# The second layer of two blocks merged into the column transform's block products

## The chip, the cores and the metric

The kernel runs on one core of one Trainium2 chip. Times are device microseconds of that core. The program of before was run twice: 861.01 and 860.78 us, median 860.89 us. Engines are named as in the profile: PE (matrix products) and PEld (its weight loads), DVE (vector), ACT (scalar), POOL (GpSimd), SP (here only an issuer of DMAs).

## The reference, cut to what matters

For 2,048 rows x of 640 columns, xn = layernorm(x), and the result is a sum of three terms:

```
a = xn @ Wd_re.T ;  b = xn @ Wd_im.T           # transform along the 640 columns
A = Ws_re @ a - Ws_im @ b                      # transform along the 2,048 rows, real part
h = gelu(xn @ w1 + b1)                         # 640 -> 1,536, tanh form of gelu
B = h @ w2 + b2                                # 1,536 -> 640
out = x + A + B
```

All inputs are float32. The kernel computes the transforms with the matrices that it is given; it does the row transform first, P = Ws_re @ xn and Q = Ws_im @ xn, and then the column transform, A = P @ Wd_re.T - Q @ Wd_im.T.

## The kernel before

**Products.** Each float32 operand is split into a high part of type fp32r and the rest. `product` (L272 to L274) issues three matmuls: high x high, high x low, low x high. A split is one ACT copy (high, L160) and one DVE subtraction (low, L161). Every matmul has a stationary 128x128 piece and 512 moving columns. Work goes by four blocks t = 0 to 3 of 512 rows.

**First part, the two-layer term (MLP).** For each block there are 12 units i of 128 hidden features. `hidden` (L292) does 15 matmuls into bank g mod 3, `gelu` (L305 to L311) activates on ACT and splits the result, and `output` does 5 x 3 matmuls with the split W2 of that unit into five banks, which add up over the 12 units. PE's order is hidden(g+2), output(g). In block 0 each unit also brings in and splits its piece of W1 and W2 (`load_w1`, four DMAs on SP, `load_w2`, one DMA; `prep_w1`, `prep_w2`), three buffers deep. `background` lays the layernorm of the next block between the units: rows of x are loaded, normalised by DVE, stored to the DRAM tensor xs (16 DMAs a block), read back turned (`load_z`, four DMAs, after all stores), transposed by DVE and split (`prep_xt`). `prep_w` makes the forms of the column transform's matrices on ACT and DVE, stores them from ACT's own DMA queue to DRAM (`wits`), three steps for each of five 128-column groups. At the end of a block b2 is added on ACT, DVE turns the result, and GpSimd adds it to x (L337); the sum waits in DRAM (`ys`).

**Second part, the row transform.** It uses seven block products in place of eight, in sequence stages of 14 entries (7 products w, 2 entries each). For each entry, `form` splits the moving operand three entries ahead into one of three places of the tile `as`, so ACT first waits until PE has done the entry that used the place.

**Third part, the column transform.** For two blocks at a time, a stage of 21 entries (7 products, 3 entries each: two pairs of 128-row chunks and one single). Its operands are the sums u and v (the two transforms of the block's rows), in seven combinations, against the forms of the Fourier matrices from `wits`, which `load_g` brings in ahead, in the last stage up to 19 forms deep. The order of the stages is: row transform of all blocks (first half), of (1,3) and (1,0), column transform of 3 and 0, row transform of (1,1) and (1,2), column transform of 1 and 2. What stands beside each entry on DVE, ACT and SP is written out by entry number in `beside` and `hidden_beside`: sums between operands, turned outputs, loads.

The order on each engine is that in which the program is written. A DMA carries one of eight semaphores, given in turn to the DMAs of SP and ACT, and is not issued until the earlier DMA with that semaphore has landed.

Of the kernel before, what the change touches and what calls it, by code (L numbers as in the profile page):

```python
# [15 lines left out]
P = 128  # L16
# [10 lines left out]
def kernel(  # L27
# [13 lines left out]

# [38 lines left out]
    NC = TB // P  # L80

# [16 lines left out]
    forms_c = dram.tile([NK, P, 2, 7 * P], F32, name="forms_c")  # L98
    parts2 = dram.tile([NT, 4, P, 2, TB], F32, name="parts2")
# [74 lines left out]
    xt = {}  # L174

    def load_x(c, eng=nc.sync):
        xt[c] = row_tile(f"x{c}")
        eng.dma_start(xt[c], x[c * P : (c + 1) * P])  # L178
# [42 lines left out]
    def new_xt(t, j):  # L221
        XT[j] = mr.tile([P, 2, TB], F32R, tag="xt", bufs=ND, name=f"xt{t}_{j}")
# [14 lines left out]
    def prep_xt(t, j):  # L237
        new_xt(t, j)
        split(XT[j][:, 0], XT[j][:, 1], zt.pop(j))
# [3 lines left out]
    def load_w1(i, eng=nc.sync):  # L243
        if i >= NF:
            return
        t = early.tile([P, ND, P], F32, tag="w1r", bufs=3, name=f"w1r{i}")
# [5 lines left out]
    def load_w2(i, eng=nc.sync):  # L252
        if i >= NF:
            return
        t = early.tile([P, D], F32, tag="w2r", bufs=3, name=f"w2r{i}")
# [24 lines left out]
    def hidden(g):  # L280
        i = g % NF
# [8 lines left out]
        for n, (j, k) in enumerate(steps):  # L290
            a, b = kinds[k]
            nc.tensor.matmul(  # L292
                acc, W1[i][:, a, j * P : (j + 1) * P], XT[j][:, b], start=n == 0, stop=n == len(steps) - 1
# [5 lines left out]
    FIRST += [(1, 1), (4, 0), (4, 2), (2, 1), (3, 1), (4, 1)]  # L299

# [116 lines left out]
    blocks = [(0, t) for t in range(NT)] + [(1, t) for t in (NT - 1, *range(NT - 1))]  # L417
# [74 lines left out]
    entries = [(*st, w, u) for st in stages for w in range(NW) for u in range(2 if st[0] == "s" else 3)]  # L492
# [4 lines left out]
    def form(n):  # L497
# [7 lines left out]
        else:  # L505
            names, which = MOV[w]
            src = sums[what[which], names[u]]
            if u < 2:
# [90 lines left out]
    warms = [early.tile([P, TB], F32R, tag="w1r", bufs=3, name=f"warm{k}") for k in range(3)]  # L599
# [18 lines left out]
    load_w2(0)  # L618
    nc.sync.dma_start(b1c, b1.rearrange("(i p) -> p i", p=P))
    load_w2(1)  # L620
    load_w2(2)

    for tag, size, keys in PLACES:
        t = place(tag, (P, size // 4))
# [42 lines left out]
    for j in range(ND):  # L667
        split(XT[j][:, 0], XT[j][:, 1], tacc[j])
    load_w1(3)
    load_w1(4)  # L670
# [5 lines left out]
    prep_w2(0)  # L676
    prep_w1(2)
    load_w2(3)
    load_w1(5)


    def background(t, i):

        if t == 1 and i == 0:
# [5 lines left out]
        if t + 1 < NT:  # L690
            c0 = (t + 1) * NC

            s = 2 if t == 0 else 0
            if t == 0 and i < 2:
                ln_apply(2 * i)
                ln_apply(2 * i + 1)
# [616 lines left out]
```

## Time and profile before

| | |
|---|---|
| median of two runs | 860.89 us |
| span of the profiled execution | 858.6 us |
| difference, outside first and last instruction | 2.3 us |
| PE busy | 850.2 us, 3,747 matmuls |
| DVE, ACT, POOL busy | 624.1, 335.7, 21.0 us |
| DMA | 152.34 MB, mean 177 GB/s |

The profiled execution is a further one, which has a span and no time of its own; the median stands 2.3 us above that span. A row of a group gives engine and line, operation, out<-in, shapes and count, then busy time and mean ns of one, then idle time ahead and what ended it. A row in order of time gives start, duration, engine, line, operation and count of merged neighbours. SPq is SP's DMA queue: the time is that of issuing, not of the transfer. A row of a stretch (A:B) gives its length, then busy time of PE, PEld, DVE, ACT and POOL with counts, the granted clock, the DMA engines' share and GB/s.

### The profile page before, as it was taken

What the parts mean: (1) busy time and instruction counts of PE and PEld (TensorE: products, weight loads), DVE (VectorE), ACT (ScalarE), POOL (GpSimd) and SP (SyncE); (2) the same over time, 40 slices, a digit from 0 to 9 for tenths busy, and PEclk for the clock granted to TensorE, in tenths of its full rate; (3) what the DMA queues carried; (4) which work ended last, traced back from release to release, by engine and by line L of the source; (5) the groups of instructions that cost most, each with busy time, mean ns of one, the idle gap of its engine ahead of it and who ended that gap; (6) DMA issues with size and microseconds to landing.
All of it is one profiled execution on the core that took longest, in us unless ns stands there. A gap on an engine that the chain in (4) does not pass through costs nothing.

```text
span 858.6 us, 10232 instructions
## 1 busy us (share of the span) xinstructions
PE 850.2 (99%) x3747; PEld 703.1 (82%) x3747; DVE 624.1 (73%) x792; ACT 335.7 (39%) x468; POOL 21.0 (2%) x22
## 2 busy tenths in 40 slices
PE   8999999999999999999999999999999999999997
PEld 6888888888888888888888888888888888888885
DVE  7554555366443678989989787998977998885687
ACT  7354434255333555443434344232322423223241
POOL 0000300030003000000000000000000000000000
PEclk9999999999999999999999999999999999999999
DMA  6656476875457984949753659954765879804364
GB/s 184 198 164 175 97 176 189 215 153 174 141 165 169 319 358 86 218 105 216 167 151 86 184 159 266 237 127 107 176 186 172 260 177 230 313 19 177 123 170 105
DMA packets 208625, 152.34 MB, mean 177 GB/s; under 512 B 82368, under 2 KB 182976, under 8 KB 208064
## 3 DMA queue, kind: packets, MB, share of 16 engines
q1 hardware_dynamic: 196336, 138.98, 62.4%
q10 hardware_dynamic: 12240, 12.72, 4.2%
q8 instruction: 29, 0.48, 0.2%
q14 instruction: 20, 0.16, 0.1%
HBM read 108.67 MB, written 42.99 MB: 177 GB/s over the span
## 4 chain that ended last, share of the span: by engine, by line
PE 98%; DMA 0%; DVE 0%; SPq 0%; issue 0%; ACT 0%; DVEq 0%; ACTq 0%
PE banks L273 26%; PE banks L272 26%; PE banks L274 26%; PE banks L292 19%; DMA x<-in_A_x_dram 0%; PE banks L635 0%; DVE st L185 0%; SPq L178 0%; DVE yo L1278 0%; DVE mv L186 0%; DVE xp L208 0%; ACT mv L192 0%; DVE mv L194 0%; DVE mv L195 0%; DVE mv L197 0%
## 5 line engine op out<-in xcount | busy, mean ns | idle before, releaser
L274 PE MATMUL banks<-as,xab 128*128 128x512 f32 x407 | 158.4, 389 | 0.0
L272 PE MATMUL banks<-as,xab 128*128 128x512 f32 x407 | 158.3, 389 | 0.0
L273 PE MATMUL banks<-as,xab 128*128 128x512 f32 x407 | 158.3, 389 | 0.0
L160 ACT ACTIVATE as<-r 128x1024 fp32r<-128x1024 f32 x80 | 85.0, 1062 | 173.1 <-PE banks L274 148.6
L161 DVE TENSOR_TENSOR as<-r,as 128x1024 fp32r<-128x1024 f32 x80 | 97.2, 1216 | 38.9 <-ACT as L160 38.9
L292 PE MATMUL banks<-xt,xab 128*128 128x512 f32 x420 | 99.1, 389 | 0.0
L311 DVE TENSOR_TENSOR hs<-ab,hs 128x512 fp32r<-128x512 f32 x48 | 36.5, 760 | 78.5 <-ACT hs L309 78.5
L292 PEld LDWEIGHTS banks<-xt,xab 128*128 128x128 f32 x420 | 78.7, 188 | 16.5 <-DVE xt L161 0.2
L272 PEld LDWEIGHTS banks<-as,xab 128*128 128x128 f32 x407 | 76.4, 188 | 16.0
L273 PEld LDWEIGHTS banks<-as,xab 128*128 128x128 f32 x407 | 76.4, 188 | 15.9
L274 PEld LDWEIGHTS banks<-as,xab 128*128 128x128 f32 x407 | 76.4, 188 | 15.8
L272 PE MATMUL banks<-as,xc 128*128 128x512 f32 x224 | 87.1, 389 | 0.0
L273 PE MATMUL banks<-as,xc 128*128 128x512 f32 x224 | 87.1, 389 | 0.0
L274 PE MATMUL banks<-as,xc 128*128 128x512 f32 x224 | 87.1, 389 | 0.0
L305 ACT ACTIVATE ab<-banks,b1c 128x512 f32<-128x512 f32 x48 | 33.0, 689 | 96.3 <-PE banks L292 91.8
L160 ACT ACTIVATE as<-rt 128x1024 fp32r<-128x1024 f32 x32 | 34.0, 1063 | 70.6 <-PE banks L274 57.9
L292 PE MATMUL banks<-xt,as 128*128 128x512 f32 x240 | 57.0, 389 | 0.0
L292 PEld LDWEIGHTS banks<-xt,as 128*128 128x128 f32 x240 | 45.0, 188 | 9.4
L272 PEld LDWEIGHTS banks<-as,xc 128*128 128x128 f32 x224 | 42.0, 188 | 8.8
L273 PEld LDWEIGHTS banks<-as,xc 128*128 128x128 f32 x224 | 42.0, 188 | 8.7
L274 PEld LDWEIGHTS banks<-as,xc 128*128 128x128 f32 x224 | 42.0, 188 | 8.7
L272 PE MATMUL banks<-hs,xc 128*128 128x512 f32 x120 | 46.7, 389 | 0.0
(170 smaller groups left out, 1365.5 us busy)
## 6 DMA issues: line engine op xcount, KB each, us to landing
raw<-in_A_dft_seq_re_dram SPq DMA_DIRECT2D x64, 256.0 KB, 5.9
raw<-in_A_dft_seq_im_dram SPq DMA_DIRECT2D x64, 256.0 KB, 5.4
wit<-wst ACTq DMA_DIRECT2D x20, 384.0 KB, 3.5
ws<-wit SPq DMA_DIRECT2D x15, 384.0 KB, 4.4
x<-in_A_x_dram SPq DMA_DIRECT2D x16, 320.0 KB, 4.3
xs<-x SPq DMA_DIRECT2D x64, 80.0 KB, 1.8
xo<-in_A_x_dram SPq DMA_DIRECT2D x16, 320.0 KB, 6.1
forms_ab<-xab SPq DMA_DIRECT2D x4, 1280.0 KB, 5.9
```

The source lines that it names most:

```text
L160: nc.scalar.activation(h, s, AF.Copy)
L161: nc.vector.tensor_tensor(l, s, h.bitcast(F32), op=ALU.subtract)
L272: nc.tensor.matmul(acc, wh, mh, start=first, stop=False, skip_group_check=goes_on)
L273: nc.tensor.matmul(acc, wh, ml, start=False, stop=False, skip_group_check=goes_on)
L274: nc.tensor.matmul(acc, wl, mh, start=False, stop=last, skip_group_check=goes_on)
L292: nc.tensor.matmul(acc, W1[i][:, a, j * P : (j + 1) * P], XT[j][:, b], start=n == 0, stop=n == len(steps) - 1)
L305: nc.scalar.activation(a, acc, AF.Gelu_apprx_tanh, bias=b1c[:, i : i + 1])
L311: nc.vector.tensor_tensor(hs[:, 1], a, hs[:, 0].bitcast(F32), op=ALU.subtract)
```

## The change

Blocks 0 and 1 no longer have an `output` in the first part. Their gelu results stay float32 and go to a new DRAM tensor hd, two units together (512 KB), from ACT's queue (`keep`). In the last column-transform stage, which now belongs to blocks 0 and 1 (the order of the last row blocks is turned about), the 12 units take part as six more 128-row chunks of contraction in each of the seven products: the first six units stand beside u, the other six beside v, and the pieces of w2 beside the real and the imaginary matrix. The stage has 42 entries, six for each product: three as before, and three with two chunks of units each (`merged_entry`).

The raw w2 is loaded during the last row-transform stage (`load_raw_w2`); the forms of w2 that the seven products need are made in the stage itself, high parts by ACT, low parts and the sums between by GpSimd (`w2_form`, `w2_sums`), in eight places (`wt`). x is added to the two blocks by loading it as the start of the output tile, b2 by GpSimd (`bias_rows`). The forms of the Fourier matrices there have 6 places in place of 19.

In the first part, blocks 0 and 1 have 15 matmuls for a unit. W1 has six raw buffers; W2's pieces are loaded and split from the end of block 1 on, one for each unit of block 2. `background` is a table by block and unit.

```
+    def keep(g, acc):
+        t, i = divmod(g, NF)
+        if i % 2 == 0:
+            HT["kept"] = mr.tile([P, 2, TB], F32, tag="hs", bufs=3, name=f"hu{g}")
+        h = HT["kept"]
+        nc.scalar.activation(h[:, i % 2], acc, AF.Gelu_apprx_tanh, bias=b1c[:, i : i + 1])
+        if i % 2:
+            nc.scalar.dma_start(hd[t, i // 2], h)
...
+            (0, 0): [lambda: apply(0, 1), lambda: stats(4)],
+            (0, 1): [lambda: apply(2, 3), lambda: stats(5), lambda: rows_in(8, 9, 10, 11)],
+            (0, 2): [lambda: stats(6, 7)],
+            (0, 3): [lambda: ln_scale(4, 4), lambda: apply(4, 5, 6, 7), lambda: load_z(1)],
...
+            (0, 10): [lambda: prep_x(1, 3, 4), lambda: rows_in(12, 13, 14, 15)],
...
+    w_steps = [(1, i) for i in (1, 2, 3, 10, 11)] + [(2, i) for i in (0, 1, 2, 3, 4, 5, 5, 6, 7, 7)]
...
+    for g in range(NM * NF):
+        t, i = divmod(g, NF)
+        acc = (acc0, acc1)[g] if g < 2 else hidden(g)
+        if t == 0:
+            prep_w1(i + 3)
+            load_w1(i + 6)
+        keep(g, acc)
+        beside_mlp(t, i)
...
+    def bias_rows(dst, c0, c1):
+        nc.gpsimd.tensor_tensor(dst, dst, A["b2"][:, c0:c1].unsqueeze(1).to_broadcast([P, NB, c1 - c0]), op=ALU.add)
...
+        for tag, n in (("xc01", 5), ("xab3", 3)):
+            r = place(tag, (P, n, 2, 3 * P))
+            A["wt"] += [r[:, k] for k in range(n)]
...
+    def w2_form(k):
+        if k >= NW * NH:
+            return
+        w, f = divmod(k, NH)
+        t = A["wt"][k % len(A["wt"])]
+        WT[w, f] = t
+        at = 0
+        for half, c0, n in W2_PARTS[w]:
+            src = w2_cols(f, half, c0, n)
+            hi, lo = (t[:, a, at * P : (at + n) * P].rearrange("p (c q i) -> p c q i", q=Q, i=B) for a in range(2))
+            nc.scalar.activation(hi, src, AF.Copy)
+            pool_add(lo, src, hi.bitcast(F32), ALU.subtract)
+            at += n
+        w2_sums(k + 4)
...
+            post = [lambda k=k: w2_form(k) for k in w2_steps(n)]
+            post += {
...
+                1: [lambda: bias_rows(ya, 0, DQ)],
+                4: [lambda: bias_rows(yo[tb, 4], 4 * B, DQ)],
...
+    def w2_steps(n):
+        if n < 4:
+            return (2 * n, 2 * n + 1)
+        w, u = divmod(n - 1, HU + NH // 2)
+        return [8 + NH * w + 2 * (u - HU) + k for k in range(2)] if u >= HU else []
```

More of the change, by code (lines that the diff above doesn't have):

```diff
@@ L254, in load_w2 @@
             return
[L255 removed]
+        t = row_tile(f"w2r{i}")
         w2r[i] = t
@@ L491, with parts_of @@
             stages.append(("y", (blocks[k - 1][1], blk[1])))
-    entries = [(*st, w, u) for st in stages for w in range(NW) for u in range(2 if st[0] == "s" else 3)]
+    HU = ND // 2 + 1
+    def parts_of(kind, what):
+        return 2 if kind == "s" else HU + NH // 2 if what == stages[-1][1] else HU
+    entries = [(*st, w, u) for st in stages for w in range(NW) for u in range(parts_of(*st))]
+    units = {}
     SRC = ("cr1", "cr2", "ci1", "cr1", "cr2", "cr1", "ci2")
@@ L1249 @@
         b = blocks.index(what) if kind == "s" else b
-        count = NW * (2 if kind == "s" else 3)
+        count = NW * parts_of(kind, what)
         for n in range(first, first + count):
```

379 lines of the change are left out of this document (278 added, 101 removed).

## The prediction

> **What bounds the kernel now.** I read the page first, then PE in order of time, the chain of waits, the DMA issue queue, and last the groups and stretches that give prices. Page, PE's first hidden units, chain:
>
> ```profile
> span 858.6 us, 10232 instructions
> PE 850.2 (99%) x3747; PEld 703.1 (82%) x3747; DVE 624.1 (73%) x792; ACT 335.7 (39%) x468; POOL 21.0 (2%) x22
> ```
> ```profile
> 12.13 10.56 PE L292 MATMUL banks<-xt,xab 128*128 128x512 f32 x45
> ```
> ```profile
> 66.89 3.40 PE banks L292 x15
> ...
> 852.85 0.24 PE banks L274
> ```
>
> PE is busy for 850.2 of 858.6 us. Hidden units start at 12.13, the last matmul stands at 852.85, and between them the chain stays on PE: 15 matmuls of one hidden unit take 3.40 us, 0.227 us each. No wait inside can be removed. Only fewer matmuls make this kernel shorter, and every new wait of PE adds its full length. The runs' median is 860.89, 2.3 us above this execution's span; I add these 2.3 at the end. Two per cent (17.2 us, about what a measurement here tells from no change) means 843.7 and 878.1.
>
> **What is removed.** The second layer of blocks 0 and 1 costs 2 x 12 chunks x 5 column blocks x 3 = 360 matmuls. In its place each of the seven products gets six more chunks of contraction: 18 block columns x 6 x 3 = 324. So 36 go, 36 x 0.227 = **-8.2 us**. Removing all else that PE lacks to 100% would bring 8.4 more, 16.6 together: faster by over 2% is out of reach.
>
> **The first block.** Before, 30 matmuls stood between two hidden units (6.8 us); now 15, in blocks 0 and 1. Unit 10 of block 0 is wanted at 12.13 + 10.56 (three units) + 7 x 3.40 = 46.5 us. Its W1 column must have come by then. It comes through SP's queue (issue start, time, count; then microseconds to landing, SP's waits, the two halves of the split, and the stretch):
>
> ```profile
> 0.74 1.83 SPq L178 DMA_DIRECT2D x<-in_A_x_dram  x4
> 5.30 5.61 SPq L250 DMA_DIRECT2D w1r<-in_B_w_dram  x12
> ...
> 19.47 3.13 SPq L672 DMA_DIRECT2D b2c<-in_B_b_dram  x4
> ...
> 49.66 0.38 SPq L257 DMA_DIRECT2D w2r<-in_B_w_dram  x1
> ...
> 62.46 7.37 SPq L203 DMA_DIRECT2D xs<-x  x16
> 71.28 1.91 SPq L229 DMA_DIRECT2D z<-xs  x4
> ```
> ```profile
> w1r<-in_B_w_dram SPq DMA_DIRECT2D x48, 80.0 KB, 3.1
> ```
> ```profile
> SPq L203 <- DMA wit<-wst: 15.9, 5, 7.7
> ```
> ```profile
> L160 ACT ACTIVATE xab<-w1r 128x640 fp32r<-128x640 f32 x6 | 4.4, 727 | 0.0
> L161 DVE TENSOR_TENSOR xab<-w1r,xab 128x640 fp32r<-128x640 f32 x6 | 4.9, 821 | 0.0
> ```
> ```profile
> 12.10:52.80 40.70, 40.70 (x182) 33.57 (x181) 23.73 (x41) 21.66 (x33) 0.00 (x0) 1.00 0.74 204
> ```
>
> In the changed program 97 DMAs stand on SP up to the last piece of this column: 12 of x, 44 of W1, b1c, 4 of b2c, 32 stores to xs, 4 of z. The W2 loads left the queue, but the xs stores of block 1, z of block 1 and x of block 2 now stand ahead of W1's last two columns; z also waits until all xs stores have landed.
>
> *Lower end.* SP at its bare pace: 16 issues in 7.37 us, 0.46 each. 0.74 + 97 x 0.46 + 1.3 (b2c, 3.13 for four) + 1.45 (z's wait: 62.46 + 7.37 to 71.28) = 48.1. The last piece lands 3.1 after its issue began: 50.7; ACT's and DVE's halves, 0.73 and 0.82: 52.3. PE waits 5.8 us.
>
> *Middle.* SP's real pace in this part of before: from 5.30 to 50.04 it issued 78 DMAs, 0.574 each, since a DMA waits on one of eight semaphores until an earlier one has landed. 0.74 + 97 x 0.574 + 1.45 = 57.9, usable 62.1: PE waits 15.6 us. The new 512 KB stores of gelu units, one for each two units, take their turn in the same eight; stores of ACT held SP up for 15.9 us in five waits before (row above).
>
> *Upper end.* Bytes: 12 x tiles 3.9 MB, 11 W1 columns 3.6, xs 2.6, z 1.3, four unit stores 2.1: 13.6 MB. At 204 GB/s, what this stretch moved before, that is 67 us, usable 69: PE waits 22 us. Were the DMA engines full (204/0.74 = 276 GB/s), 49 us: 5 us of waiting, the lower end again.
>
> I take **13 us**, nearer to SP's real pace than to the bare one. Behind the waiting copy on ACT stands gelu of unit 7, whose bank unit 10 needs at that very moment, so nothing more is lost; unit 11's column follows four DMAs (about 2 us) later, inside unit 10's 3.40. Later nothing gives this time back, as PE has no other slack.
>
> **After the wait.** PE idles there for longer than anywhere in the trace of before.
>
> ```profile
> 1.91 7.03 PE L616 MATMUL banks<-warm 128*128 128x512 f32 x19 [1.91 <-DVE warm L607]
> ```
>
> The 19 warming matmuls took 7.03 us where 19 x 0.227 = 4.3 would do: a start from rest cost up to 2.7 us. A restart costs 0 to 2.7; I take **1**, the idle time coming in pieces. The Trainium skill, "TensorE: Matmul & The Clock Gate", section "Part 1: The HAM clock gate", says the array clock halves after an idle window of about 3.4 us and needs as much sustained work to return; by that each such gap would cost about 1.7 us, an estimate from that page; the stretch above reads a clock of 1.00, and no run here shows such a gap yet.
>
> **Block 1.** Gelu without the split (one activation for two, no DVE) frees ACT, but three steps of forming W (prep_w) now stand in three units of 3.40 us; before, a unit of 6.8 had one or two.
>
> ```profile
> L160 ACT ACTIVATE wst<-wt 128x256 fp32r<-128x256 f32 x35 | 14.3, 414 | 42.2 <-DMA wit<-wst 25.1 <-DVE wt L354 11.0 <-DVE wt L414 5.4
> ```
>
> ACT stands at these copies for their own stores (25.1 us over the run), and gelu is queued behind them. Three banks let PE run two units (6.8 us) ahead of gelu. Two rounds of store and reuse, some 3.5 us each, and the copies between come to about 8 us within that time: 0 to 4 us; I take **1**.
>
> **The merged stage.** It has 270 + 324 = 594 matmuls, 594 x 0.227 = 134.7 us. Its loads come in the last sequence stage:
>
> ```profile
> 275.00:320.00 45.00, 45.00 (x200) 37.24 (x200) 29.18 (x70) 23.94 (x49) 0.00 (x0) 1.00 1.03 352
> 743.00:792.00 49.00, 49.00 (x218) 40.58 (x217) 37.36 (x35) 15.40 (x15) 0.00 (x0) 1.00 0.32 120
> ```
>
> Eleven pieces of units (5.8 MB, the last three just after the boundary) and W2 (3.9 MB) on top of 120 GB/s make about 320; 352 has been moved. I cost that at nothing; if PE waits for it, 0 to 3 us.
>
> GpSimd makes all 42 low halves of W2's forms, the sums between them, and adds b2 to blocks 0 and 1.
>
> ```profile
> L337 POOL TENSOR_TENSOR xo<-xo,ot 128x512 f32<-128x512 f32 x15 | 20.2, 1382 | 248.2 <-DVE ot L335 172.7 <-DMA xo<-in_A_x_dram 75.5
> ...
> L160 ACT ACTIVATE as<-r 128x1024 fp32r<-128x1024 f32 x80 | 85.0, 1062 | 173.1 <-PE banks L274 148.6 <-DVE u L414 9.1 <-DVE r L474 7.0
> L161 DVE TENSOR_TENSOR as<-r,as 128x1024 fp32r<-128x1024 f32 x80 | 97.2, 1216 | 38.9 <-ACT as L160 38.9
> ...
> L414 DVE TENSOR_TENSOR u<-u,u 128x512 f32<-128x512 f32 x4 | 2.7, 683 | 0.0
> ```
>
> At 1.382/512 = 2.7 ns an element, its 100 additions (25,856 elements a lane) take 69.8 us of 134.7: enough on the whole, tight at the start. The forms' places are free only when the stage begins. ACT first waits for entry 0 (18 matmuls, 4.1 us), splits 1.06, then makes two high halves (0.41 + 0.30 each); the same after entry 1 (8.2 us): form 3 is done at 8.2 + 1.06 + 1.42 + 1.04 = 11.7. Next on GpSimd stands b2 onto 2,560 elements, 6.9 us: 18.6. Form 4 follows at 19.6; PE wants its low half at 81 matmuls + 2, 18.8. That is a wait of 0.8 us, plus what DVE's ports take from GpSimd, up to four DVE additions of 1.22: 0.8 to 5.7. I take **3**.
>
> Later forms have six entries of lead. What is left is contention:
>
> ```profile
> 95.52 0.69 DVE L311 TENSOR_TENSOR hs<-ab,hs 128x512 fp32r<-128x512 f32 x1 [5.74 <-ACT hs L309]
> ...
> 183.94 1.12 DVE L311 TENSOR_TENSOR hs<-ab,hs 128x512 fp32r<-128x512 f32 x1
> ...
> 181.97 6.75 POOL L337 TENSOR_TENSOR xo<-xo,ot 128x512 f32<-128x512 f32 x5 [75.47 <-DMA xo<-in_A_x_dram]
> ```
>
> The same DVE addition takes 0.69 alone and 1.12 while GpSimd adds. In products 3 and 4 DVE has 12 additions in 14.8 us of PE time (about 13.5 us); half of GpSimd's 8.4 us there, put on top, makes it some 3 us late against a lead of two entries. 0 to 13.3 (below); I take **1.5**.
>
> **Sum.** -8.2 + 13 + 1 + 1 + 3 + 1.5 = +11.3; span 869.9, and with 2.3 around it **872.2 us**, 1.3% slower.
>
> **Rivals.** *Ports as the bound (slower by over 2%).* In the merged stage DVE's additions of two SBUF operands are 35 x 1.216 + 7 x 0.683 (splits), 18 x 1.216 + 3 x 0.683 (operand sums) and 4 x 1.216 + 3 x 0.683 (outputs): 78.2 us. If they and GpSimd's 69.8 exclude each other, the stage takes 148.0 instead of 134.7: +13.3 in place of my 4.5, time 881.0. It decides once the two overlap in nothing. For it: 0.69 becoming 1.12. Against: of 1.35 us of GpSimd's op the DVE op lost only 0.43, and both engines have idle time to shift into. The Trainium skill, "SBUF — State Buffer", section "Who interferes with whom", states just this exclusion for a DVE instruction with two SBUF inputs against a GpSimd instruction that reads SBUF; the trace agrees in kind (0.69 to 1.12), and by the page the time would be 881, by the rows 872.
>
> *The DMA engines as the bound in the first block.* The upper end of 22 us: 858.6 + 2.3 - 8.2 + 22 + 6.5 = 881. For it: the share of 0.74 before. Against: larger packets in xs and units than in W1.
>
> *Everything at its lower end (not slower).* SP at the bare pace, 5.8 us, and 0.8 in the merged stage: 860.9 - 8.2 + 6.6 = 859.3. It decides if SP never waits for a semaphore of its own DMAs. Against: it did so through the same stretch before.
>
> *The change gives what it removes*: W1 arrives in time, 852.7. That needs the 97 issues done by about 42 us, where the bare pace takes 48.
>
> **How the numbers follow.** Forecast (864 to 878) 0.56; ports 0.12; DMA bound 0.14; lower end 0.16; full gain 0.02. The range, 857 to 888, reaches from the lower end to both slower rivals with their terms added up. Slower by over 2%: the two slower rivals, 0.26; within 2% 0.73; faster by over 2% 0.01.
>
> **What would show it.** PE's first long gaps should stand before hidden units 8 to 10, near 40 to 63 us, released by DVE or ACT and behind them by the DMA of w1r; SP issuing without pause until about 58. Another wait of a few us about 18 us into the merged stage, released by GpSimd. 3,711 matmuls. DVE's split there longer than 1.22 on average. I am wrong if PE has no gap in block 0, or if the merged stage lasts over 141 us.

## The result and the profile after

The changed kernel takes 909.7 us (908.75 to 910.65 in two runs) against 860.89 before: 1.057 times as long, with a 95% interval of 1.054 to 1.060. The prediction was 872.2 with a range of 857 to 888: the direction holds, the size doesn't. The profiled execution lasts 910.65, its span 908.8 us. Page of the kernel after, the span, the engines, and the shares of its chain:

```profile
span 908.8 us, 10404 instructions
...
PE 860.7 (95%) x3711; PEld 702.4 (77%) x3711; DVE 670.3 (74%) x791; ACT 355.4 (39%) x527; POOL 128.2 (14%) x112
...
PE 66%; DMA 11%; POOL 6%; DVE 6%; issue 4%; ACT 3%; SPq 2%; ACTq 0%; DVEq 0%; POOLq 0%
```

The 36 matmuls are gone (3,747 to 3,711). But PE is 95% busy where it was 99%, and the chain, which stayed on PE, now runs through DMAs, GpSimd, VectorE and issues for a third of the span. Stretches of the kernel after: blocks 0, 1, 2 and 3 of the MLP (180, 180, 360 and 360 matmuls, a few more where one crosses an edge) and the merged stage (594). Columns: stretch, length, busy time of PE, PEld, DVE, ACT and GpSimd with their instructions, granted clock, DMA share, GB/s.

```profile
13.59:76.26 62.67, 46.93 (x183) 37.20 (x182) 31.07 (x63) 22.86 (x35) 0.00 (x0) 0.84 0.83 220
76.26:122.39 46.13, 42.97 (x182) 34.81 (x181) 21.23 (x51) 17.94 (x32) 0.00 (x0) 0.96 0.77 225
122.39:218.62 96.23, 86.34 (x362) 69.30 (x361) 53.35 (x115) 43.39 (x89) 0.00 (x0) 0.96 0.65 186
218.62:300.22 81.60, 81.60 (x362) 67.57 (x361) 51.51 (x103) 42.84 (x79) 6.73 (x5) 1.00 0.76 235
753.09:904.30 151.21, 140.49 (x594) 110.92 (x592) 117.21 (x84) 59.74 (x113) 120.75 (x100) 0.99 0.35 100
```

A stretch's loss is its length less its matmuls times 0.2267 us: 62.67 - 40.81 = 21.9 in block 0, then 5.3, 14.6, 0.0, and 151.21 - 134.66 = 16.5 in the merged stage. Nothing was lost between 300 and 753. With -8.2 for the matmuls, 1.2 for a later first hidden unit and -1.0 for a shorter tail this makes +50.3; the spans differ by 50.2. So four places carry everything: blocks 0, 1 and 2 and the merged stage.

PE's waits in the kernel after (waiting line, releaser: us in all, times, longest):

```profile
PE banks L274 <- ACT hu L289: 18.9, 4, 11.0
PE banks L255 <- DVE as L139: 7.0, 9, 2.0
PE banks L254 <- ACT r L138: 4.7, 1, 4.7
PE banks L254 <- ACT hs L301: 3.8, 1, 3.8
PE banks L256 <- POOL xc L1173: 2.4, 1, 2.4
```

Hidden units (L274) wait for a bank that a gelu frees, output units (L254) for a W2 copy and a gelu, the merged stage for DVE's splits and once for GpSimd. What ACT's gelus stood behind in block 0, from the timeline (start, duration, instruction, idle before it and releaser):

```profile
44.03 9.61 SPq L182 DMA_DIRECT2D xs<-xc  x16
...
45.95 9.66 PE L274 MATMUL banks<-xt,as 128*128 128x512 f32 x30 [4.77 <-ACT hu L289]
...
55.28 1.91 SPq L211 DMA_DIRECT2D z<-xs  x4
57.23 6.97 SPq L232 DMA_DIRECT2D w1r<-in_B_w_dram  x8
...
63.99 1.30 DVE L215 STREAM_TRANSPOSE zt<-z 128x512 f32<-128x512 f32 x2 [15.62 <-DMA z<-xs]
65.21 0.74 ACT L138 ACTIVATE as<-w1r 128x640 fp32r<-128x640 f32 x1 [17.12 <-DMA w1r<-in_B_w_dram]
...
66.58 9.61 PE L274 MATMUL banks<-xt,as 128*128 128x512 f32 x30 [10.97 <-ACT hu L289]
```

SP issues W1's last two columns at 57 us, behind sixteen row stores and z; ACT stands 17.1 us at the copy, with the gelus queued behind it, and DVE 15.6 us at z. PE is idle for 4.8 and 11.0 us. After each idle time the next 30 matmuls take 9.6 us, where 30 x 0.227 = 6.8 would do. Stretches around the two gaps, columns as above:

```profile
44.80:51.60 6.80, 5.65 (x14) 4.45 (x15) 2.65 (x5) 2.41 (x4) 0.00 (x0) 0.51 0.71 200
...
58.50:72.20 13.70, 5.62 (x14) 4.40 (x15) 7.61 (x13) 4.87 (x8) 0.00 (x0) 0.51 1.06 246
```

The granted clock is 0.51 for 6.8 and for 13.7 us, begun during the idle time and ended 5.6 us after PE resumed, both times. Those 5.6 us at half the clock are the 2.8 us, so each of these gaps costs its length and 2.8 us more.

In block 2 the two long gaps (3.8 and 4.7 us) stand behind form steps. Before the longer one ACT waits for a step's own stores, with the copy of W2 queued behind it, and PE for that copy:

```profile
188.64 0.42 ACT L138 ACTIVATE wst<-wt 128x256 fp32r<-128x256 f32 x1 [3.83 <-DMA wit<-wst]
...
190.11 0.74 ACT L138 ACTIVATE r<-w2r 128x640 fp32r<-128x640 f32 x1 [1.06 <-DVE wst L139]
...
190.90 0.50 PE L254 MATMUL banks<-hs,r 128*128 128x512 f32 x1 [4.70 <-ACT r L138]
```

In the merged stage GpSimd and DVE stretch each other. Timeline, then groups by form:

```profile
766.84 5.71 POOL L1122 TENSOR_TENSOR yo<-yo,xc 128x2560 f32<-128x2560 f32 x1 [0.19 <-POOL xc L1173]
...
768.43 6.87 DVE L139 TENSOR_TENSOR as<-v,as 128x1024 fp32r<-128x1024 f32 x2 [2.79 <-ACT as L138]
```
```profile
L1173 POOL TENSOR_TENSOR xc<-xab,xc 128x256 fp32r<-128x256 f32 x27 | 34.1, 1269 | 533.3 <-ACT xc L1216 533.3
...
L139 DVE TENSOR_TENSOR as<-r,as 128x1024 fp32r<-128x1024 f32 x8 | 12.0, 1498 | 8.8 <-ACT as L138 8.7
```

Beside the b2 addition two splits take 6.87 us, where two of 1.22 were usual; in the whole stage this split takes 1.50 (1.22 before), and GpSimd needs 1.27 us for 256 elements.

### The profile page after: what moved, and what is told of

It is laid out like the page before. It is cut to its first block, busy times and chain, and to the rows that moved or that the text cites. A ratio compares the mean times of both kernels' runs of the same rounds, so it can differ in the third digit from the quotient of the medians.

```text
span 908.8 us, 10404 instructions
## 1 busy us (share of the span) xinstructions
PE 860.7 (95%) x3711; PEld 702.4 (77%) x3711; DVE 670.3 (74%) x791; ACT 355.4 (39%) x527; POOL 128.2 (14%) x112
## 4 chain that ended last, share of the span: by engine, by line
PE 66%; DMA 11%; POOL 6%; DVE 6%; issue 4%; ACT 3%; SPq 2%; ACTq 0%; DVEq 0%; POOLq 0%
PE banks L256 20%; PE banks L255 20%; PE banks L254 20%; PE banks L274 6%; DMA wit<-wst 4%; POOL xab L1173 4%; POOL xc L1173 2%; DMA w1r<-in_B_w_dram 2%; DVE as L139 2%; DMA w2r<-in_B_w_dram 2%; DMA hd<-hu 1%; DMA z<-xs 1%; SPq L182 1%; DVE wst L139 1%; DVE wt L346 1%
## 5 line engine op out<-in xcount | busy, mean ns | idle before, releaser
L255 PE MATMUL banks<-as,xab 128*128 128x512 f32 x391 | 152.8, 391 | 0.3 <-DVE as L139 0.3
L256 PE MATMUL banks<-as,xab 128*128 128x512 f32 x391 | 152.8, 391 | 0.0
L254 PE MATMUL banks<-as,xab 128*128 128x512 f32 x391 | 152.6, 390 | 0.0
L139 DVE TENSOR_TENSOR as<-r,as 128x1024 fp32r<-128x1024 f32 x88 | 109.1, 1241 | 47.8 <-ACT as L138 47.6
L1173 POOL TENSOR_TENSOR xc<-xab,xc 128x256 fp32r<-128x256 f32 (+1 forms) x42 | 47.2, 1145 | 533.3 <-ACT xc L1216 533.3
L255 PE MATMUL banks<-as,xc 128*128 128x512 f32 x293 | 114.8, 392 | 3.3 <-DVE as L139 3.2
L256 PE MATMUL banks<-as,xc 128*128 128x512 f32 x293 | 114.4, 390 | 2.4 <-POOL xc L1173 2.4
L254 PE MATMUL banks<-as,xc 128*128 128x512 f32 x293 | 114.2, 390 | 0.0
L255 PEld LDWEIGHTS banks<-as,xab 128*128 128x128 f32 x391 | 73.7, 188 | 16.5 <-DVE as L139 1.2
L256 PEld LDWEIGHTS banks<-as,xab 128*128 128x128 f32 x391 | 73.6, 188 | 15.7 <-POOL xab L1173 0.5
L254 PEld LDWEIGHTS banks<-as,xab 128*128 128x128 f32 x391 | 73.7, 188 | 15.2
L274 PE MATMUL banks<-xt,xab 128*128 128x512 f32 x315 | 73.5, 390 | 0.0
L255 PEld LDWEIGHTS banks<-as,xc 128*128 128x128 f32 x293 | 55.1, 188 | 17.5 <-DVE as L139 6.3
L274 PEld LDWEIGHTS banks<-xt,xab 128*128 128x128 f32 x315 | 59.0, 188 | 12.4 <-DVE xt L139 0.2
L256 PEld LDWEIGHTS banks<-as,xc 128*128 128x128 f32 x293 | 55.0, 188 | 14.0 <-POOL xc L1173 2.9
L254 PEld LDWEIGHTS banks<-as,xc 128*128 128x128 f32 x293 | 55.1, 188 | 11.5
L274 PE MATMUL banks<-xt,as 128*128 128x512 f32 x180 | 47.8, 424 | 15.7 <-ACT hu L289 15.7
L139 DVE TENSOR_TENSOR as<-rt,as 128x1024 fp32r<-128x1024 f32 x40 | 51.1, 1277 | 12.8 <-ACT as L138 12.8
L274 PEld LDWEIGHTS banks<-xt,as 128*128 128x128 f32 x180 | 37.3, 209 | 24.9 <-ACT hu L289 16.6
L1173 POOL TENSOR_TENSOR xab<-xab,xab 128x256 f32<-128x256 f32 (+3 forms) x48 | 55.1, 1174 | 0.9 <-ACT xab L1216 0.9
```

The costliest lines, as they stand in the source:

```text
L139: nc.vector.tensor_tensor(l, s, h.bitcast(F32), op=ALU.subtract)
L254: nc.tensor.matmul(acc, wh, mh, start=first, stop=False, skip_group_check=goes_on)
L255: nc.tensor.matmul(acc, wh, ml, start=False, stop=False, skip_group_check=goes_on)
L256: nc.tensor.matmul(acc, wl, mh, start=False, stop=last, skip_group_check=goes_on)
L274: nc.tensor.matmul(acc, W1[i][:, a, j * P : (j + 1) * P], XT[t, j][:, b], start=n == 0, stop=n == len(steps) - 1)
L1173: nc.gpsimd.tensor_tensor(dst, a, b, op=op)
```

## The experiments

Each kernel ran once, beside the kernel before (860.2 to 861.3). Losses in us by stretch, from each trace as above:

| kernel | total | block 0 | 1 | 2 | 3 | merged |
|---|---|---|---|---|---|---|
| changed kernel | 909.7 | 21.9 | 5.3 | 14.6 | 0.0 | 16.5 |
| W1 by GpSimd's queue | 912.5 | 19.4 | 2.1 | 20.2 | 0.0 | 16.8 |
| form steps spread | 906.6 | 22.2 | 11.3 | 0.0 | 4.5 | 16.8 |
| b2 by VectorE | 906.3 | 21.4 | 4.1 | 16.5 | 0.0 | 12.8 |
| no low halves, no sums | 899.7 | 22.2 | 6.2 | 14.5 | 0.0 | 3.6 |
| transposes late | 904.7 | 12.0 | 5.5 | 18.9 | 0.0 | 16.6 |
| z early | 900.7 | 2.5 | 13.6 | 13.7 | 0.0 | 17.3 |
| low halves by VectorE | 904.9 | 20.9 | 3.4 | 17.0 | 0.0 | 12.5 |
| no sums of units | 902.3 | 21.6 | 2.8 | 18.9 | 0.0 | 6.7 |
| form steps late | 936.9 | 21.9 | 5.9 | 27.2 | 13.2 | 16.7 |
| late columns by GpSimd | 902.6 | 21.6 | 2.9 | 18.0 | 0.0 | 8.6 |
| all edits | 891.9 | 5.6 | 10.8 | 8.6 | 6.1 | 6.8 |
| z from x | 905.0 | 10.8 | 10.9 | 14.2 | 0.0 | 17.7 |
| all late users behind | 902.8 | 0.2 | 9.4 | 21.0 | 3.8 | 16.6 |
| block 1's loads by GpSimd | 893.9 | 0.2 | 17.9 | 2.2 | 3.9 | 17.2 |
| matrices first | 878.1 | 0.2 | 7.0 | 5.1 | 4.1 | 9.1 |

Six rows, the first among them, run blocks 0 to 2 as the changed kernel does: 20.9 to 22.2, 2.8 to 6.2 and 14.5 to 18.9. Differences within such a band are not read. A block's stretch ends with the first matmul of the next, so a wait for the next block's first unit counts in the block before it. Six of these kernels leave a part of the computation out, as their texts say: the two that lack sums, and the last four.

### Blocks 0 to 2: which late thing?

**W1 by GpSimd's queue.**

```diff
-            load_w1(i + 6)
+            load_w1(i + 6, nc.gpsimd)
```

> Edit: from the seventh column on, W1 is loaded from GpSimd's DMA queue, so that it no longer stands behind the xs stores and z on SP. In the changed kernel block 0 takes 62.7 us for 40.8 us of matmuls, 21.9 lost (16.8 idle, the rest at the halved clock). Theory (the order and pace of SP's queue): the loss falls to 6 us or less, span about 893. Rival (the DMA engines are full there, share 0.70 to 1.02 between 30 and 75 us): W1 comes no sooner or something else comes later, the loss stays over 15 us, span over 902.

By its numbers this is the rival's outcome (19.4 us lost, 912.5). The gap before unit 8 went, that before unit 10 grew to 17.1 us. DVE and PE in the timeline:

```profile
63.93 1.30 DVE L215 STREAM_TRANSPOSE zt<-z 128x512 f32<-128x512 f32 x2 [22.26 <-DMA z<-xs]
...
67.12 5.19 PE L274 MATMUL banks<-xt,as 128*128 128x512 f32 x15 [17.14 <-DVE as L139]
```

The column has come, but its low half is queued on DVE behind two transposes of z, which waited 22.3 us for their load. W1's place in SP's queue, the prediction's cause, was one of two waits that end together (65.2 and 64.0 us in the changed kernel).

**Form steps spread.**

```diff
-    w_steps = [(1, i) for i in (1, 2, 3, 10, 11)] + [(2, i) for i in (0, 1, 2, 3, 4, 5, 5, 6, 7, 7)]
+    w_steps = [(1, i) for i in (1, 3, 5, 7, 9)] + [(2, i) for i in range(10)]
```

> Edit: the fifteen steps that form the column matrices stand in other units: 1, 3, 5, 7, 9 of block 1 and 0 to 9 of block 2, never two in one unit, never in neighbouring units of block 1. Blocks 1 and 2 lose 5.3 and 14.6 us now. Theory (ACT stands at its two buffers until its own stores have landed, 28.1 us there, and gelu and W2's copies are queued behind): together they lose 8 us or less, span about 897. Rival (W2's loads come late through SP's queue, behind z): they still lose 14 us or more, span over 903.

Block 2's 14.6 us went to nothing, as the stretch shows:

```profile
128.20:209.80 81.60, 81.60 (x362) 67.57 (x361) 50.52 (x110) 41.19 (x81) 0.00 (x0) 1.00 0.69 200
```

So block 2 has no lack of capacity. Block 1 lost more: ACT stood 11.2 us at a copy behind block 2's z transposes, and block 3 lost 4.5. Together blocks 1 and 2 lost 11.3, between the theory's 8 and the rival's 14.

**Transposes late**: the run with W1 by GpSimd's queue, and block 1's transposes and splits all at (0, 11), behind every W1 column.

```diff
-            (0, 6): [lambda: turn_z(1, 0, 1), lambda: stats(9)],
...
+            (0, 11): [
+                lambda: turn_z(1, 0, 1),
+                lambda: prep_x(1, 0),
...
```

> The W1 columns from the 7th on go by GpSimd's queue, as in the run before with that edit, and the five transposes and splits of block 1's z move behind every W1 column of block 0 (all at (0, 11)); nothing is left out. Theory A (with the W1 columns early, what stopped hidden unit 10 at 49.8 us for 17.3 us was the order on DVE: the two transposes of z, whose load lands at about 63.5 us, stand ahead of the low half of W1 column 10, and the late thing is z itself): the gap before unit 10 goes, block 0 loses under 4 us where it lost 19.4, and the same lateness comes back before the first unit of block 1, as one gap of 12 to 18 us; blocks 0 and 1 together lose 16 to 22, against 21.6; total 909 to 914. Theory B (the W1 columns or the hidden-unit stores are late by themselves, and the transposes only stood beside them): block 0 keeps a gap over 8 us before units 9 to 11.

As theory A says, the wait moved to block 1's first unit, at 53.9 us: 11.3 us. PE's wait for it:

```profile
PE banks L274 <- ACT rt L138: 11.3, 1, 11.3
```

The table has this wait in block 0. Blocks 0 and 1 lose 17.5 together, within its 16 to 22 (the total, 904.7, is under its 909 to 914). z itself was late.

**z early.**

```diff
-            nc.sync.dma_start(xs[c % NC * NC + k, c // NC * B : (c // NC + 1) * B], xt[c][k * B : (k + 1) * B])
+            (nc.sync, nc.gpsimd)[k % 2].dma_start(xs[c % NC * NC + k, c // NC * B : (c // NC + 1) * B], xt[c][k * B : (k + 1) * B])
...
-            (0, 1): [lambda: apply(2, 3), lambda: stats(5), lambda: rows_in(8, 9, 10, 11)],
+            (0, 1): [lambda: apply(2, 3), lambda: stats(5)],
```

> As the run with the transposes moved behind the W1 columns, and z of block 1 is brought forward: the loads of block 2's four x tiles go behind z's load (SP spent 6.7 us on them ahead of block 1's stores of normalised rows), and every second store of normalised rows is issued by GpSimd's queue instead of SP's (SP spent 11.4 us on sixteen). Nothing is left out. Theory A (the time at which z of block 1 lands, set by SP's issues one behind another, is what block 0 or block 1 waits for): z lands 10 to 17 us earlier, at 46 to 53 us, and blocks 0 and 1 together lose 2 to 9 us where they lost 21.6 (27.2 in the changed kernel); total 893 to 901 with the rest as it was. Theory B (z is late because the 16 DMA engines are full in this stretch, or because the normalising comes late on DVE, whichever queue issues): it lands less than 5 us earlier, and the two blocks lose over 15.

The kernel also issues W1's last columns sooner and moves the statistics of block 2's rows to block 1. z was in use from 55.7 us on, 8 earlier, and block 0 lost 2.5. But block 1 lost 13.6, so together 16.1: neither theory as it stood. ACT in block 1:

```profile
91.11 0.42 ACT L138 ACTIVATE wst<-wt 128x256 fp32r<-128x256 f32 x1 [5.10 <-DMA wit<-wst]
92.02 0.52 ACTq L369 DMA_DIRECT2D wit<-wst  x1
92.59 1.27 ACT L289 ACTIVATE hu<-banks,b1c 128x512 f32<-128x512 f32 x2 [1.06 <-DVE wst L139]
```

Now the gelus stand behind a form step that waits for its own store.

**Form steps late.**

```diff
+    w_steps = [(2, i) for i in (4, 4, 5, 5, 6, 6, 7, 7, 8, 8, 9, 9, 10, 10, 11)]
```

> The fifteen steps that make the column transform's matrix forms (prep_w) all move to units 4 to 11 of block 2, two in a unit; blocks 0 and 1 and the first four units of block 2 run without them. Nothing is left out. Theory A (the gaps of blocks 1 and 2 are gelus and W2 copies on ScalarE that stand behind a step's copies, which wait for a DMA load or for the store that frees their buffer; two hidden units of 3.4 us give half the slack that two units of 6.8 us gave before): block 1 loses under 1.5 us where it lost 5.3, the gap before block 2's first output (4.0 us at 132.4) goes, block 2 may lose up to 15 in its later units, where the steps now stand two by two. Theory B (the gaps of block 1 come from block 2's z or from hidden-unit stores): block 1 still loses over 3 us.

Block 1 still lost 5.9, without one form step in it. ACT there:

```profile
108.85 0.63 ACT L138 ACTIVATE xt<-zt 128x512 fp32r<-128x512 f32 x1 [12.24 <-DVE zt L215]
```

Here theory B held: block 2's z. With two steps in a unit block 2 then lost 27.2 us, where up to 15 was allowed, and block 3, for which nothing was said, 13.2.

**z from x.** z of blocks 1 and 2 no longer waits for the normalised rows.

```diff
+            if t < 3:
+                v = rows_of(x, t)[:, :, q * DQ : (q + 1) * DQ]
```

> The W1 columns from the 7th on by GpSimd's queue, and z of blocks 1 and 2 is read from x itself, without waiting for the normalised rows: block 1's at (0, 0), block 2's first at (1, 0). Left out: the normalising of these two blocks' rows as the hidden units see them; all statistics, normalising and stores of normalised rows are still done. Theory A (blocks 0 and 1 lose because x rows, statistics, normalised stores, z's load, transposes and splits are a chain that takes longer than the 40.8 us which a block of hidden units alone lasts, where it had 81.6 before): blocks 0 and 1 together lose under 5 us, against 21.6 with the W1 columns by GpSimd alone and 27.2 in the changed kernel; total 892 to 899, block 2 and the last stage losing 14 to 20 each as before. Theory B (queues, DMA engines or ScalarE's order cost the same whenever z comes): the two blocks lose 10 us or more.

21.7 us were lost all the same: the long chain to z was not all that held these blocks, and theory A fell. In z's place on DVE stood the statistics of block 2's rows:

```profile
50.69 0.88 DVE L164 BATCH_NORM_STATS2 st<-x 128x6 f32<-128x320 f32 x2 [15.65 <-DMA x<-in_A_x_dram]
```

**All late users behind.** The same with these statistics at (0, 11), form steps one to a unit and W2 copies two units ahead.

```diff
-            (0, 5): [lambda: stats(8)],
...
+            (0, 11): [lambda: stats(8, 9, 10, 11)],
...
-            prep_w2(i + 1)
+            for k in (1, 2) if i == 0 else (i + 2,):
+                prep_w2(k)
```

> As the run with z of blocks 1 and 2 read from x (the normalising of these two blocks is again left out of what the hidden units see), and every other late transfer whose user stands ahead of block 0's or 1's work on an in-order engine is put behind that work: the statistics of block 2's rows go to (0, 11), behind all W1 columns; the form steps go one to a unit, three in block 1 (units 7, 9, 11) and twelve in block 2; W2 copies run two units ahead. The number of operations and bytes stays. Theory A (each engine has time enough in blocks 0 to 2, and what PE loses there are in-order queues: an instruction whose transfer is late holds the gelu, W1 half or W2 copy queued behind it): block 0 loses under 2.5 us, blocks 0 and 1 together under 6 where they lost 21.7, block 2 under 5; total 882 to 892. Theory B (ScalarE, VectorE or the DMA engines are full at half the time per unit, so that any order loses about as much): blocks 0 to 2 together lose over 18 us.

Block 0 ran through:

```profile
12.95:53.95 41.00, 41.00 (x183) 33.76 (x182) 27.17 (x51) 22.90 (x35) 14.18 (x24) 1.00 0.84 236
```

It lost 0.2 us with the same work on ACT as in the changed kernel (22.9 us) and the same DMA share (0.84 against 0.83). So the engines have time enough for block 0's own work, and its 22 us came from late transfers and from what stood queued behind them. About the DMA engines this run alone says less, since it moves fewer bytes in block 0 (9.7 MB by length and rate, 13.8 in the changed kernel). *All edits*, below, says more: its block 0 moves 13.2 MB in 46.4 us, 284 GB/s, and loses 5.6. Blocks 1 and 2 missed theory A by far, and the three together lost 30.6, over theory B's mark. SP's queue, DVE in block 1, and SP's waits:

```profile
28.50 23.38 SPq L182 DMA_DIRECT2D xs<-x  x16
...
73.64 10.81 SPq L213 DMA_DIRECT2D z<-in_A_x_dram  x4
...
88.92 1.30 DVE L217 STREAM_TRANSPOSE zt<-z 128x512 f32<-128x512 f32 x2 [22.97 <-DMA z<-in_A_x_dram]
```
```profile
SPq L182 <- DMA hd<-hu: 29.0, 7, 6.8
SPq L213 <- DMA hd<-hu: 10.9, 2, 9.0
```

Sixteen stores, 7.37 us before, held SP for 23.4. By the releasers that the profile infers, SP was waiting for the new stores of gelu units (hd) to land, with which it shares the eight semaphores: 29.0 us at its row stores, 16.3 of them within these sixteen, and 9.0 in one wait of block 2's z loads. So block 2's z was issued only from 73.6 to 84.4, and DVE stood 23 us at it. The next run takes z away from SP.

**Block 1's loads by GpSimd.** Block 2's z, row stores and the W2 rows by its idle queue.

```diff
+            (nc.gpsimd if t == 2 else nc.sync).dma_start(z[q * B : (q + 1) * B], v)
...
-    def load_w2(i, eng=nc.sync):
+    def load_w2(i, eng=nc.gpsimd):
```

> As the run before with all late users behind block 0's work (z of blocks 1 and 2 read from x, so the normalising of these two blocks is left out of what the hidden units see), and GpSimd's queue, idle from 32 us on, takes over what came late in block 1: z of block 2 (issued at (0, 10)), the stores of block 2's normalised rows, and the w2 rows, the first three at (1, 0). The form steps of block 1 stand at units 4, 6 and 8. Theory A (what PE lost in blocks 1 and 2 were again late transfers, here 51 to 105 us of SP's queue full of row stores, whose users held the gelus): block 1 loses under 3 us where it lost 9.4, block 2 under 7 where it lost 21.0; total 870 to 886. Theory B (ScalarE and VectorE have too much to do there, or the DMA engines): blocks 1 and 2 together still lose over 15 us.

Block 2 held to theory A (2.2). But block 1 lost 17.9, so the two together 20.1, over theory B's 15, and the total of 893.9 missed theory A's. PE's longest wait, 9.5 us, stood behind one more late load:

```profile
91.27 0.84 DVE L348 STREAM_TRANSPOSE wt<-wraw 128x640 f32<-128x640 f32 x1 [18.27 <-DMA wraw<-in_A_dft_hid_re_dram]
```

**Matrices first.** Block 3's rows behind that load, and the merged stage as in *late columns by GpSimd*, below.

```diff
-            (0, 10): [lambda: prep_x(1, 3, 4), lambda: load_z(2), lambda: rows_in(12, 13, 14, 15)],
+            (0, 10): [lambda: prep_x(1, 3, 4), lambda: load_z(2)],
```

> As the run before with GpSimd's queue for what came late in block 1 (again without the normalising of blocks 1 and 2 in what the hidden units see), but the loads of block 3's x rows go from (0, 10) to (1, 6), so that SP issues the matrix loads of the first form step ahead of them, and the form steps of block 1 stand at units 6, 8 and 10; the last stage has its low halves and b2 additions as in the run that kept only the late columns' additions on GpSimd. Theory A (the 9.7 us before block 1's ninth unit were one more late transfer: the matrix load, issued at 81 to 90 us behind block 3's rows, for which the step's transposes waited 18 us with the gelus queued behind): block 1 loses under 4 us where it lost 17.9, blocks 0 and 2 stay under 1 and 4, the last stage loses 6 to 9; total 866 to 874, so still over the kernel before. Theory B (block 1 has too much to do for its 40.8 us): it loses over 8 us in other places.

Block 1 lost 7.0, between the theories. Block 2 (5.1), the last stage (9.1) and the total (878.1) came out over theory A's marks too. Block 1's second half:

```profile
74.00:94.00 20.00, 17.76 (x78) 14.45 (x77) 5.81 (x11) 5.24 (x11) 6.76 (x14) 0.98 1.01 290
```

ACT and DVE are busy for 5 to 6 of 20 us, but the DMA engines have no room (1.01): here the remaining wait, 2.2 us and again behind the matrix load, may be throughput. The other, 2.6 us at 68 us, stands behind the statistics of block 2's rows. That wasn't separated further. Nor does any run take the unit stores (hd) off the semaphores that they share with SP.

### The merged stage: GpSimd or DVE?

**b2 by VectorE.**

```diff
-        nc.gpsimd.tensor_tensor(dst, dst, A["b2"][:, c0:c1].unsqueeze(1).to_broadcast([P, NB, c1 - c0]), op=ALU.add)
+        nc.vector.tensor_tensor(dst, dst, A["b2"][:, c0:c1].unsqueeze(1).to_broadcast([P, NB, c1 - c0]), op=ALU.add)
```

> Edit: b2 is added to the two blocks by DVE instead of GpSimd. The merged stage takes 151.2 us for 134.7 us of matmuls, 16.5 lost; its first gap, at 771.7 us, stands behind GpSimd's addition of 2,560 elements (5.71 us, in which two DVE splits took 6.87 us). Theory (that long addition sets the first gap, the many short ones the later gaps near 830 to 880): the first gap of 2.6 us and the slow clock after it go, 4 to 5 us, and with 5,120 elements less on GpSimd the later ones shrink by a few more: stage about 143. Rival (the first gap is due to the late raw w2 or to ACT): the gap stays, stage over 148.

The wait 18 us into the stage, where the prediction had placed it, went. The stage took 147.4, between the theory's 143 and the rival's 148: 12.8 us remained, one wait of 4 us among them new, behind an addition on DVE whose columns had not landed.

**No low halves, no sums** on GpSimd.

```diff
-            pool_add(lo, src, hi.bitcast(F32), ALU.subtract)
+            if k < len(A["wt"]):
+                nc.gpsimd.memset(lo.bitcast(F32), 0.0)
```

> Edit: GpSimd's low halves and sums of W2's forms are left out (the low halves are zero, the combined columns are not formed; the output is not the reference's); b2 stays on GpSimd. Theory (GpSimd, by its own time and by the ports it shares with DVE, is all that the merged stage waits for): the stage takes 135 to 138 us, of which the b2 addition at its start may cost up to 3. Rival (DVE alone cannot make the splits and sums of 42 entries in time, or the loads of units and Fourier forms come late with 6 places): over 142.

Stretch, and DVE's split by form:

```profile
754.64:892.89 138.25, 135.19 (x594) 110.95 (x592) 95.44 (x84) 57.97 (x107) 15.88 (x12) 1.00 0.38 109
```
```profile
L139 DVE TENSOR_TENSOR as<-r,as 128x1024 fp32r<-128x1024 f32 x8 | 9.8, 1224 | 9.7 <-ACT as L138 9.5
```

DVE's same 84 instructions take 95.4 us instead of 117.2, the split 1.22 again, and the loss is 3.6 (the stage, 138.25, is at the upper end of the theory's 135 to 138): GpSimd's low halves and sums cost some 13 us.

**No sums of units**: twelve of DVE's additions left out.

```diff
-            return lambda: add(op(1, 0, k), op(1, 0, k), op(0, 0, k), ALU.subtract)
+            return lambda: k < HU and add(op(1, 0, k), op(1, 0, k), op(0, 0, k), ALU.subtract)
```

> The twelve additions and subtractions by which DVE combines the kept hidden units (the parts t1 to t4 with k from 3 on) are left out, about 18 us of DVE's 117 in 150 us; the products take the units as they are, so the output is not the reference's. GpSimd keeps all its work. Theory A (the two engines take turns, and it is the sum of their work that is too long): GpSimd's 128x256 operation shortens from 1.15 to under 1.05 us, and the stage loses 3 to 9 us in place of 16.5, of which about 2 to 3 before the first gelu entry for the b2 addition; total 895 to 903. Theory B (GpSimd's own pace, whatever DVE does): its operations stay at 1.15 us, and the stage loses 14 us or more.

6.7 lost, inside theory A's 3 to 9. But GpSimd's operation went only from 1.27 to 1.21 us, not under 1.05. PE's waits for DVE's splits, 7.0 us in the changed kernel, are 0.8 here and 1.2 without GpSimd's low halves: what PE meets is mostly DVE's lateness, and relieving either engine takes it away.

**Low halves by VectorE**, with the b2 additions.

```diff
-            pool_add(lo, src, hi.bitcast(F32), ALU.subtract)
+            add(lo, src, hi.bitcast(F32), ALU.subtract)
```

> VectorE does the b2 additions and all low halves of the w2 forms in the last stage; GpSimd keeps only the sums of w2's pieces (20 in the changed kernel's program, by products 2 to 5). Nothing is left out. Theory A (GpSimd is slow there because it and DVE take turns at the SBUF, so that work on GpSimd costs more time than the same work on DVE): a 128x256 low half takes about 0.42 us on DVE (the same shape takes that in the MLP stage) where GpSimd takes 1.15, DVE is busy for 125 to 137 us of the stage's 140, and the stage loses 2 to 7 us where it lost 16.5 (12.8 with the b2 additions alone on DVE); total 893 to 900. Theory B (DVE is full, and its order decides; more work on it makes the operands later still): the stage loses 14 us or more.

A low half takes 0.46 us there, near the 0.42 expected, and DVE's sum goes only from 117 to 120 us with 70 instructions more. But 12.5 were lost, between the two marks:

```profile
845.45 1.22 DVE L1122 TENSOR_TENSOR u<-u,xc 128x1024 f32<-128x1024 f32 x1 [1.16 <-DMA u<-in_A_x_dram]
848.89 1.22 DVE L1122 TENSOR_TENSOR u<-u,xc 128x1024 f32<-128x1024 f32 x1 [2.22 <-DMA u<-in_A_x_dram]
850.04 1.22 DVE L139 TENSOR_TENSOR as<-xc,as 128x1024 fp32r<-128x1024 f32 x1
```

The split that PE wants at 846.6 stands behind two b2 additions, and these behind a load.

**Late columns by GpSimd**: the same, but these two additions on GpSimd.

```diff
-            bias_rows(dst, c0, c1)
+            bias_rows(dst, c0, c1, nc.gpsimd)
```

> In the last stage VectorE makes the low halves of the w2 forms and adds b2 to the output tiles, as in the run with the low halves on VectorE, but GpSimd keeps the b2 additions to the late columns, which wait for a load issued just before them. Nothing is left out. Theory A (what was left at 846.6 us in that run, 4.7 us and the slow matmuls behind it, was VectorE's queue standing behind an addition whose load had not landed): that gap goes, the stage loses 3 to 7 us where it lost 12.5; total 895 to 901 with the rest as in the changed kernel. Theory B (VectorE has too much work there in any order): over 10 us are lost.

```profile
846.57 14.42 POOL L1122 TENSOR_TENSOR u<-u,xc 128x1024 f32<-128x1024 f32 x2 [18.39 <-DMA u<-in_A_x_dram]
```

That gap went, and 8.6 were lost, 1.6 above theory A's range. GpSimd now takes 14.4 us for the two additions beside a busy DVE (6.7 in the changed kernel).

**All edits** in one kernel, with the whole computation kept; beside the diffs above:

```diff
+            (1, 0): [lambda: ln_scale(8, 4), lambda: apply(8, 9, 10, 11), lambda: load_z(2), open_w],
...
+            load_w(0, 0, nc.gpsimd)
+            load_w(1, 0, nc.gpsimd)
...
+    w_steps = [(1, i) for i in (4, 6, 7, 8)] + [(2, i) for i in range(11)]
```

> All edits that helped in one kernel: W1 columns and half of the normalised rows' stores by GpSimd's queue, block 2's x rows by that queue behind them, the transposes of z behind the W1 columns, the matrix loads of the first step by GpSimd's queue, the fifteen form steps spread over block 1 (four) and block 2 (one in a unit), W2 copies two units ahead, and the last stage as with the late columns' additions on GpSimd. Nothing is left out. Theory A (the loss is the sum of waits that each come from the order of queues, so that the edits add up): start and block 0 lose 3 to 6 us together, block 1 under 5, block 2 and 3 under 4 together, the last stage 3 to 7; the total is 862 to 876. Theory B (the waits share one limit, the DMA engines' or VectorE's throughput, and come back elsewhere when one goes): over 880.

891.9: over theory B's mark. The merged stage held (6.8), start and block 0 lost 7.7 (a first unit 2.1 us later than before, and 5.6), and blocks 1 to 3 lost 25.5. That waits come back elsewhere is as theory B says; that they share one limit isn't shown, as the DMA share was 0.77, 0.60 and 0.76 there. No kernel tried beats the one before; even without normalising in z's way *matrices first* takes 878.1.

## Why the prediction was wrong

In the spans, +11.3 was forecast and +50.2 came. Of the difference block 2 is 14.6 us, the merged stage 12.0, the first block with its restarts 7.9, block 1 4.3.

- **-8.2 for 36 matmuls**: right, 3,711 remained at 0.227.
- **First block, 13 (5.8 to 22)**: 21.9. Place and cause were as said: the bank's gelu behind the copy of W1, W1 behind the xs stores and z. The *middle* case, SP's real pace, came near: last piece of the column issued at 57.9 by the sum, at 58.8 in the trace's chain. That its 15.6 us of waiting meets the measured 4.8 + 11.0 is partly luck: the sum has one gap, the trace two, and the piece took 6.3 us to land where 3.1 was put. The step that failed is the choice of 13, below the middle, towards a bare pace that the queue kept only in places. What the prediction didn't see: z was as late, so moving W1 alone did not help (19.4 lost). The rival with the DMA engines as the bound had 22 us, and that it meets 21.9 is luck too: its 204 GB/s were no limit, as *all edits* moved 284 in this block.
- **After the wait, 1 (0 to 2.7)**: 30 matmuls in 9.6 us twice, 2.8 each, in block 0 alone 5.6. The row on the warming matmuls gave 2.7, and that was the value to take, once for each gap; that the idle time would come in pieces was no reason for less. The Trainium skill, "TensorE: Matmul & The Clock Gate", section "Part 1: The HAM clock gate", has the half clock after an idle window and a busy window to get back; the trace agrees in kind (0.51), and shows more than the 1.7 us that the prediction estimated from that page (2.8).
- **Block 1, 1 (0 to 4)**: 5.3, and 2.8 to 6.2 in kernels with the same order. The wait that it placed is there, 2.2 us behind a form step; a second, 1.0 us, stands behind block 2's z, which had no term, and slow matmuls after the first make up the rest. Without any form step in block 1 it still lost 5.9: taking one wait away uncovered the other.
- **Block 2**: no term, 14.6 measured. This is the largest miss. The change also moved the form steps of block 2 and put W2's copies behind them, and the prediction followed them no further than block 1. Spread evenly, they cost nothing there in the one run that changed only this; in later kernels with one step to a unit block 2 lost 2.2 to 21.0, so spreading alone doesn't settle it.
- **Merged stage, start 3 and contention 1.5 (0.8 to 5.7, 0 to 13.3)**: 16.5. The first wait was right in place, releaser and size (2.4 us, 18 us in). The contention term failed: it put half of GpSimd's work in products 3 and 4 on top of DVE's and counted on slack for the rest. But the two engines slowed each other over the whole stage: the same 84 DVE instructions took 117.2 us, and 95.4 without GpSimd's low halves and sums. The rival *ports as the bound* came nearest, with the stage at 148.0; it took 151.2. Its condition, that the two overlap in nothing, isn't shown. The Trainium skill, "SBUF — State Buffer", section "Who interferes with whom", says that two-operand work of DVE and GpSimd's reads take turns; the trace agrees in kind (a split of 1.22 us takes 1.50 on average). GpSimd's 69.8, estimated from one row of before, became 120.8 us busy; how much of that is its own pace no run shows, since DVE was busy beside it in all of them.
- **Loads in the last sequence stage, 0**: right, nothing was lost between 300 and 753 us. **Start**, taken as unchanged: 1.2 later, but 0.2 to 1.4 in seven further kernels with the same start, so its size is mostly scatter.
- Rivals on the other side (859.3, 852.7) had the bare pace or a punctual W1 as their point of decision; neither was met. What the prediction named as its refutation happened: the merged stage lasted over 141 us. The gaps stood before units 8 and 10 as named. The range failed because all four places missed upwards together: each wait was priced in one place, as if the rest would stand still.

## What to carry to other kernels

When a stage's unit is halved, a transfer has half the time to arrive before PE meets its lateness (3.4 us for 6.8 here); list all users of DMAs that stand ahead of the critical work in each queue, since removing one wait only uncovers the next. Ask also which transfers share a semaphore: a store that waits for its gelu can hold a queue that has nothing to do with it. Price each gap of PE with its restart. For work given to GpSimd beside a VectorE as busy as here (117 of 151 us), adding the two engines' two-operand work came nearest (148.0 for 151.2).

## What was not expected of the hardware

A wait of 4.8 us and one of 11.0 cost the same on top, 2.8 us, though the half clock was granted for 6.8 and 13.7 us: in both, 5.6 us of it lay behind the wait. The stretching of GpSimd and VectorE goes both ways and isn't even: a 2,560-element GpSimd addition (5.71 us) made two DVE splits take 6.87 us where 2.4 was usual, while beside an almost unbroken row of DVE instructions two GpSimd additions of 1,024 elements took 14.4 us where they had taken 6.7. Sixteen row stores of 80 KB held SP's queue for 7.4 us before and for 23.4 in the run with all late users behind; the DMA engines weren't full for most of that (share 1.10 up to 35 us, 0.67 to 45, 0.43 to 52), and 16.3 us of it were waits for the unit stores.
